# Turning every probability tile by DMA in an attention and MLP block on one Trainium2 core

## The chip, the core and the metric

The kernel runs on one NeuronCore of a Trainium2 chip. Its metric is the device time of one execution in microseconds (us). Three executions of the kernel before took 2775.61, 2779.23 and 2780.73 us, median 2779.23. Comparisons with a changed kernel tell about 0.2% from nothing.

A core has five engines that run their own instruction queues in order: TensorE (PE; its weight loads are listed as PEld), VectorE (DVE), ScalarE (ACT), GpSimd (POOL) and SyncE (SP, which here only issues DMAs). They wait for one another by semaphores. SBUF is the on-chip memory; PSUM holds what TensorE writes.

## The reference

A transformer block over 2048 rows of 576 numbers, modulated by a condition vector `c`:

```python
mod = (silu(c) @ w_mod).reshape(1, 6, 1, 576)
sa, ca, ga, sb, cb, gb = (mod[:, k] for k in range(6))
h = layernorm(x) * (1 + ca) + sa
q = (h @ wq).reshape(1, 2048, 32, 128)         # 32 heads, 16 key/value heads, two heads share one
s = einsum("bhqd,bhkd->bhqk", q, k_last_512) * 128 ** -0.5
o = einsum("bhqk,bhkd->bhqd", softmax(s), v_last_512)
x = x + ga * (o @ wo)
h = layernorm(x) * (1 + cb) + sb
x = x + gb * ((silu(h @ w1) * (h @ w3)) @ w2)  # 4608 hidden columns
```

Everything is fp32 in memory.

## The kernel before

**Precision.** A matrix product is made of fp16 halves: a scaled fp32 value is split into a high half (its fp16 rounding) and a low half (what is left), and a product is high x high + high x low + low x high, three matmuls. Every split costs a copy to fp16 (on ScalarE) and a subtraction (on POOL or VectorE).

**Attention, in slots.** A slot is one head on one block of 512 rows: 32 x 4 = 128 slots, in an order in which most key/value groups do all four blocks at once and some do two and come back later (`uses`, `slots`). Slots come in pairs (`j` = 0 and 1): the two heads of a key/value group on the same block. A slot `i` has four quarters `t`, one for each tile of 128 rows. The loop that starts with `for i in range(n + 2)` writes the work of several slots out in one fixed order, and every engine keeps that order. In slot `i`, quarter `t`, it issues among others:

- `scores(i, t)`: three matmuls (128 x 512) into a PSUM bank of tag "S" (two banks), then VectorE's maximum over each row and the bias for the exponential;
- `weights(i, t)`: ScalarE's exponential `p` of tile `t`, with the row sums into `l`;
- for tiles 0 to 2, `half_high` (ScalarE copies `p` to fp16) and `half_low` (POOL subtracts), both into the tile `hp`, and two quarters later `turn_away`: one DMA transpose on SP's queue writes both halves, turned, into a quarter of `ptw`;
- for tile 3, in quarter 1 of the next slot, `turn`: four 128 x 128 transposes on TensorE into a bank of tag "T", then `turn_high` (ScalarE) and `turn_low` (VectorE) write the halves into `ptw`;
- a third of the next slot's query product (`query`), two groups of the output product of a pair two slots back (`attend_out`, into the bank `E`), and prepared tasks.

At the end of slot `i` `values(i - 1)` makes the value product of the slot before: twelve matmuls, each over all four turned tiles, into a bank of tag "A". So a tile of slot `i - 1` has to be turned by the end of slot `i`.

**The softmax denominator.** `sums` takes the reciprocals of the row sums (VectorE), stores them to DRAM (`row`) and loads them back spread over all partitions (`r`), since the value product comes out with rows along the free axis. `normalize` multiplies, `split_on` makes the halves of the result (copy on ScalarE, subtraction on POOL). `attend_out` sums both heads of the pair in `E` and adds them to `acc` with a scale per key/value group.

**Other work in the slots.** From slot 13 to 123 the MLP's weights are combined, split and stored, mostly on ScalarE and POOL, spread over the quarters (`step_of`); so are the attention's own weights, keys and values (`step_at`). These tasks run in `run(i, t)`, after the quarter's own work. The blocks' normalized rows are turned and modulated (`make_h`) in slots 0 to 1, 8 to 9 and 11 to 12. The MLP (`mlp`) begins in the last slots and fills the rest of the time.

**The opening.** Before slot 0 stand: the loads of the first block, two tables of `w_mod`, two heads of `wq` and one of the keys; the norm; `weigh_mod` and `mod_cols`, which multiply the tables with silu(c) in rows and sum them over partitions by matmuls with ones; peaks and scales (`scale_first`, `scales`); `modulate` for the five chunks of the first block; the first query.

**Buffers.** Every tag has a fixed number of buffers, and a writer waits until the reader of the tile that held its buffer is done: `p` 4, `hf` (with `hp`) 4, `ptw` 2, `raw` 3.

## Time and profile before

| | |
|---|---|
| median of three runs | 2779.23 us |
| profiled execution | 2777.58 us, span 2775.8 us |
| granted TensorE clock | 0.993 |
| busy | PE 2688.3, DVE 1998.5, POOL 1864.7, ACT 1622.7 us |
| bytes moved by DMA | 463 MB |
| first scores / last value product | 38.8 / about 1618 us |

The span is the time from the first to the last instruction of the program; the execution's own time is 1.8 us longer. In the views a row of the timeline is: start and length in us, engine, line, operation, tile written <- tiles read, shapes. A row of groups is: line, engine, operation, tiles, shapes, count | busy us, mean ns of one | idle time of the engine just before them and what ended most of it. A row of waits is: who waited <- for whom: us in total, times, longest. Matmul rows that overlap are merged; their length holds the drain of the pipeline.

### The profile page before, as it was taken

What the parts mean: (1) busy time and instruction counts of PE and PEld (TensorE: products, weight loads), DVE (VectorE), ACT (ScalarE), POOL (GpSimd) and SP (SyncE); (2) the same over time, 40 slices, a digit from 0 to 9 for tenths busy, and PEclk for the clock granted to TensorE, in tenths of its full rate; (3) what the DMA queues carried; (4) which work ended last, traced back from release to release, by engine and by line L of the source; (5) the groups of instructions that cost most, each with busy time, mean ns of one, the idle gap of its engine ahead of it and who ended that gap; (6) DMA issues with size and microseconds to landing.
All of it is one profiled execution on the core that took longest, in us unless ns stands there. A gap on an engine that the chain in (4) does not pass through costs nothing.

```text
span 2775.8 us, 44765 instructions
## 1 busy us (share of the span) xinstructions
PE 2688.3 (97%) x15412; PEld 1513.3 (55%) x15412; DVE 1998.5 (72%) x3556; ACT 1622.7 (58%) x3022; POOL 1864.7 (67%) x1731
## 2 busy tenths in 40 slices
PE   5899999999999999999999999999999999999998
PEld 3455555555555555555555555555555555555555
DVE  7777788877787787887876667777776666566666
ACT  4687777777777878777677635544443333333332
POOL 3567788888788877777669637688873465333435
PEclk8999999999999999999999999999999999999999
DMA  5878778778786888879878935656643434333332
GB/s 164 176 170 190 189 185 188 179 179 189 169 186 165 188 197 189 215 179 208 190 190 223 238 115 170 196 168 201 210 145 108 160 121 128 105 102 110 104 110 78
DMA packets 594420, 463.25 MB, mean 167 GB/s; under 512 B 443152, under 2 KB 472976, under 8 KB 593424
## 3 DMA queue, kind: packets, MB, share of 16 engines
q1 hardware_dynamic: 593584, 460.39, 65.0%
q8 instruction: 121, 1.98, 0.3%
q14 instruction: 107, 0.88, 0.1%
q10 hardware_dynamic: 608, 0.00, 0.0%
HBM read 263.60 MB, written 95.99 MB: 130 GB/s over the span
## 4 chain that ended last, share of the span: by engine, by line
PE 52%; DVE 2%; issue 1%; ACT 1%; POOL 0%; DMA 0%; DVEq 0%; ACTq 0%; POOLq 0%; SPq 0%
PE py L770 15%; PE px L770 11%; PE pe L855 7%; PE pf L855 7%; PE pe L359 3%; PE po L485 3%; PE pss L406 3%; PE pq L348 2%; PE pt L446 0%; PE pq L352 0%; DVE table L410 0%; DVE acc L513 0%; DVE u L955 0%; DVE acc L866 0%; DMA row<-l 0%
## 5 line engine op out<-in xcount | busy, mean ns | idle before, releaser
L460 POOL TENSOR_TENSOR hp<-p,hp 128x512 f16<-128x512 f32 x384 | 448.0, 1169 | 281.0 <-ACT hp L455 156.8
L423 ACT ACTIVATE p<-pss,table,factors 128x512 f32<-128x512 f32 x512 | 396.7, 775 | 357.9 <-DVE table L411 178.2
L770 PEld LDWEIGHTS <-wset 128*128 128x128 f16 x3528 | 344.3, 98 | 336.8 <-issue 3.4
L410 DVE TENSOR_REDUCE table<-pss 128x1 f32<-128x512 f32 x512 | 350.3, 684 | 211.2 <-PE pss L406 207.0
L770 PE MATMUL py<-hset,wset 128*128 128x512 f16 x2016 | 482.4, 379 | 0.0
L359 PE MATMUL pe<-o 128*128 128x288 f16 x3072 | 458.8, 286 | 16.4 <-DVE acc L513 13.9
L406 PE MATMUL pss<-k,qT 128*128 128x512 f16 x1536 | 418.3, 380 | 12.3 <-ACT p L423 9.9
L359 PEld LDWEIGHTS <-o 128*128 128x128 f16 x3072 | 300.3, 98 | 190.1 <-issue 23.4
L485 PE MATMUL po<-ptw,v 128*128 128x512 f16 x1536 | 358.7, 381 | 11.7 <-DVE ptw L475 7.1
L770 PE MATMUL px<-hset,wset 128*128 128x512 f16 x1512 | 361.5, 379 | 1.6 <-ACT p L423 1.6
L348 PE MATMUL pq<-hT,wq 128*128 128x512 f16 x1092 | 281.4, 380 | 1.1 <-DVE hT L216 1.1
L92 POOL TENSOR_TENSOR akv<-u,akv 128x512 f16<-128x512 f32 x141 | 164.8, 1178 | 173.9 <-ACT akv L91 166.0
L455 ACT CAST hp<-p 128x512 f16<-128x512 f32 x384 | 237.4, 618 | 13.1 <-POOL hT L218 0.6
L485 PEld LDWEIGHTS <-v 128*128 128x128 f16 x1536 | 147.6, 98 | 176.5 <-issue 21.0
L855 PEld LDWEIGHTS <-akv 128*128 128x128 f16 x1728 | 169.6, 98 | 93.8 <-issue 4.7
L406 PEld LDWEIGHTS <-qT 128*128 128x128 f16 x1536 | 147.7, 98 | 126.7 <-issue 15.4
L513 DVE SCALAR_TENSOR_TENSOR acc<-pe,factors,acc 128x576 f32<-128x576 f32 x256 | 207.8, 812 | 10.4 <-PE pe L359 10.4
L505 POOL TENSOR_TENSOR o<-on,o 128x512 f16<-128x512 f32 x128 | 150.1, 1173 | 55.8 <-ACT o L504 53.4
L348 PEld LDWEIGHTS <-wq 128*128 128x128 f16 x1104 | 108.6, 98 | 138.5 <-issue 9.0
L849 DVE SCALAR_TENSOR_TENSOR acc<-pf,table,acc 128x576 f32<-128x576 f32 x140 | 113.5, 811 | 80.3 <-PE pf L855 80.3
L950 ACT COPY u<-py 128x512 f32<-128x512 f32 x72 | 42.1, 585 | 202.2 <-PE py L770 200.3
L943 ACT ACTIVATE s<-s,table 128x512 f32<-128x512 f32 x72 | 52.0, 722 | 174.2 <-DVE s L942 174.2
(230 smaller groups left out, 4780.3 us busy)
## 6 DMA issues: line engine op xcount, KB each, us to landing
wset<-wd SPq DMA_DIRECT2D x213, 320.0 KB, 3.2
r<-row SPq DMA_DIRECT2D x128, 256.0 KB, 4.1
oset<-od SPq DMA_DIRECT2D x106, 288.0 KB, 3.2
wraw<-in_w SPq DMA_DIRECT2D x36, 768.0 KB, 5.6
wd<-wmade SPq DMA_DIRECT2D x75, 320.0 KB, 3.3
wset<-wd SPq DMA_DIRECT2D x71, 160.0 KB, 2.3
w2raw<-in_w SPq DMA_DIRECT2D x19, 576.0 KB, 5.1
wd<-ring SPq DMA_DIRECT2D x33, 320.0 KB, 2.9
```

The lines of the kernel that those rows point to most:

```text
L92: eng.tensor_sub(halves[:, 1], src, halves[:, 0])
L348: nc.tensor.matmul(ps, w[:, k // 2, m, :], hT[:, DC + m if k == 1 else m, :], start=s == 0, stop=False)
L359: nc.tensor.matmul(E[:, h, :HALF], o[:, x, rows], w[:, y, h * HALF : (h + 1) * HALF], start=first and n == 0, stop=last and n == 2,)
L406: nc.tensor.matmul(pss, q[:, x, rows], k[:, y, :], start=n == 0, stop=n == 2)
L410: nc.vector.tensor_reduce(nm[:, 0:1], pss, axis=AX.X, op=ALU.max, negate=True)
L423: nc.scalar.activation(p, pss, AF.Exp, bias=nm[:, 1:2], scale=factor, accum_out=st["l"][:, t : t + 1])
L455: nc.scalar.copy(hp[:, 0, :], state[i]["p", t])
L460: nc.gpsimd.tensor_sub(hp[:, 1, :], state[i].pop(("p", t)), hp[:, 0, :])
L485: nc.tensor.matmul(po, v[:, x, c, :], pt[:, y, c, :], start=c == 0 and n == 0, stop=c == KC - 1 and n == 2)
L513: nc.vector.scalar_tensor_tensor(a, E[:, :, :HALF], factors[:, uses[u][0], 2:3], a, op0=ALU.mult, op1=ALU.add)
L770: nc.tensor.matmul(ps, w[:, a, :], h[:, b, :], start=start and n == 0, stop=stop and n == 6, skip_group_check=True)
L855: nc.tensor.matmul(ps[:, h, :HALF], a[:, rows], w[:, b, :], start=m == 0, stop=m == 2)
```

## The change

It has five parts.

1. **Tile 3 is turned by DMA too.** `turn`, `turn_high` and `turn_low` are gone. `half_high` runs for all four tiles, and `turn_away` has four transposes a slot, those of tiles 2 and 3 in quarters 0 and 1 of the next slot.
2. **The low half is a quarter later.** `half_low(i, t - 1)` stands at the start of quarter `t`, behind the tasks of quarter `t - 1`; that of tile 3 at the start of the next slot.
3. **Scores in four banks.** The two "T" banks are free of `turn`; even tiles' scores go there, odd tiles' to "S".
4. **A ratio of sums for a pair.** Head 0 of a pair is no longer divided by its row sum: `take_first` (ScalarE) and one VectorE instruction split its value product straight from PSUM. Head 1 is multiplied with the ratio of the two sums; the store and the spread by DMA happen for this head alone. The division by head 0's sum moves into the factor of `attend_out`, a column per tile.
5. **The opening.** The two tables come in turned by the host (`w_cols`) with `c` repeated in all partitions, so that the modulation vectors are sums along the free axis (`weigh_col`); two heads of `wq` and the keys load ahead of the second table. The peaks of the weights are found before it, TensorE runs matmuls on unused data (`warm`), half of the normalized rows are made on ScalarE. `modulate_first` makes all high halves first, and `project_first` multiplies with them first. For the other blocks `modulate` makes one fp32 result and lets POOL make both halves.

On TensorE, in quarter 1 of the slot whose first scores start at 809.58 us of the profile: before (`pt` is the turned tile's bank, `pe` the bank E, `o` and `qT` halves of the output and the query),

```order
L359 LDWEIGHTS o
L359 MATMUL pe<-o 128x288
L446 MATMUL pt<-ident,p 128x128 x4
L406 LDWEIGHTS qT
L406 MATMUL pss<-k,qT 128x512
```

and now

```order
L434 LDWEIGHTS o
L434 MATMUL pe<-o 128x288
L484 LDWEIGHTS qT
L484 MATMUL pss<-k,qT 128x512
L484 LDWEIGHTS qT
```

The four transposes are gone and the scores follow the output product at once.

On POOL, around the last quarter of the slot whose fourth scores start at 984.89 us: before (`hp` are low halves, of tile 2 first and of the next slot's tile 0 last; `wraw` and `wmade` are MLP weights, `o` the split of an attention output),

```order
L460 TENSOR_TENSOR hp<-p,hp 128x512
L685 TENSOR_TENSOR wraw<-wraw 128x384
L686 TENSOR_TENSOR wraw<-wraw 128x384
L687 TENSOR_TENSOR wraw<-wraw 128x384
L505 TENSOR_TENSOR o<-on,o 128x512
L692 TENSOR_TENSOR wmade<-wraw,wmade 128x2x256
L693 TENSOR_TENSOR wmade<-wraw,wmade 64x2x128
L695 TENSOR_TENSOR wraw<-wraw 128x384
L460 TENSOR_TENSOR hp<-p,hp 128x512
```

and now, from the low half of tile 1 on,

```order
L531 TENSOR_TENSOR hp<-p,hp 128x512
L769 TENSOR_TENSOR wraw<-wraw 128x384
L770 TENSOR_TENSOR wraw<-wraw 128x384
L771 TENSOR_TENSOR wraw<-wraw 128x384
L531 TENSOR_TENSOR hp<-p,hp 128x512
L589 TENSOR_TENSOR o<-on,o 128x512
L776 TENSOR_TENSOR wmade<-wraw,wmade 128x2x256
L777 TENSOR_TENSOR wmade<-wraw,wmade 64x2x128
L779 TENSOR_TENSOR wraw<-wraw 128x384
L531 TENSOR_TENSOR hp<-p,hp 128x512
```

The low half of tile 2 has moved behind three weight instructions, and that of tile 3, which is new, stands behind the output's split and three more.

On SP's queue, from the same slot as the first place on: before (`ptw` a turned tile, `row` and `r` the reciprocals out and back, `od` MLP weights, `oraw` and `wraw` loads),

```order
L467 DMA_TRANSPOSE ptw<-hp 128x8x128
L642 DMA od_172<-omade 128x1152
L436 DMA r<-row_9460 128x512
L467 DMA_TRANSPOSE ptw<-hp 128x8x128
L287 DMA oraw<-in_wo 128x1152
L467 DMA_TRANSPOSE ptw<-hp 128x8x128
```

and now

```order
L538 DMA_TRANSPOSE ptw<-hp 128x8x128
L350 DMA oraw<-in_wo 128x1152
L538 DMA_TRANSPOSE ptw<-hp 128x8x128
L726 DMA od_175<-omade 128x576
L538 DMA_TRANSPOSE ptw<-hp 128x8x128
L516 DMA row_9204<-l 128x4
```

Four transposes a slot stand there, and a `row` with its `r` in every second slot.

The core of the diff:

```diff
-        pss = bank("S", "pss")
+        pss = bank("S", "pss") if t % 2 else t_bank()
...
     def sums(i, step):
 
+        u, j, b = slots[i]
         st = state[i]
+        if j == 0:
+            return
+        first, both, up, ratio = (st["l"][:, lo * ST : hi * ST] for lo, hi in ((0, 1), (0, 2), (2, 4), (4, 5)))
         if step == 0:
-            nc.vector.reciprocal(st["l"][:, ST:], st["l"][:, :ST])
+            nc.vector.reciprocal(up, both)
+            nc.vector.scalar_tensor_tensor(ratio, first, O_DOWN, up[:, ST:], op0=ALU.mult, op1=ALU.mult)
         elif step == 1:
             st["row"] = dram.tile([P, ST], F32, name=f"row{i}")
-            nc.sync.dma_start(st["row"], st["l"][:, ST:])
+            nc.sync.dma_start(st["row"], ratio)
...
+    def take_first(i):
+        st = state[i]
+        o = st["o"] = new_o(i)
+        nc.scalar.activation(o[:, 0, :], st["po"], AF.Copy, scale=O_DOWN)
+
     def normalize(i):
         st = state[i]
         po = st.pop("po")
+        if slots[i][1] == 0:
+            o = st["o"]
+            nc.vector.scalar_tensor_tensor(o[:, 1, :], po, O_DOWN, o[:, 0, :], op0=ALU.mult, op1=ALU.subtract)
+            return
...
-        for h in (high, hf):
-            if on_vector:
-                nc.vector.tensor_scalar(h, ps, g, s, op0=ALU.mult, op1=ALU.add)
-            else:
-                nc.scalar.activation(h, ps, AF.Identity, bias=s, scale=g)
-        eng = nc.vector if on_vector else nc.gpsimd
+        if on_vector:
+            nc.vector.tensor_scalar(hf, ps, g, s, op0=ALU.mult, op1=ALU.add)
+        else:
+            nc.scalar.activation(hf, ps, AF.Identity, bias=s, scale=g)
+        nc.gpsimd.tensor_copy(high, hf)
...
+    def weigh_col(wm, k, m, on_vector):
+        w, to = wm[m], mod_a[:, k, m : m + 1]
+        if on_vector:
+            nc.vector.scalar_tensor_tensor(w, w, 1.0, c_row, op0=ALU.mult, op1=ALU.mult, accum_out=to)
+        else:
+            nc.gpsimd.tensor_mul(w, w, c_row)
+            nc.scalar.activation(w, w, AF.Copy, accum_out=to)
...
     load_x(0)
-    load(wms, 0, load_mod, 0, wrest[:, 0])
-    load(wms, 1, load_mod, 1, wrest[:, 1])
+    load(wms, 0, load_cols, 0, wrest[:, 0])
     load(wqs, (0, 0), load_in, wq, 0)
     load(keys, 0, load_kv, k_cache, 0)
     load(wqs, (0, 1), load_in, wq, 1)
+    load(wms, 1, load_cols, 1, wrest[:, 1])
...
         for t in range(ST):
+            if t and i < n:
+                half_low(i, t - 1)
+            if t == 0 and 1 <= i <= n:
+                half_low(i - 1, ST - 1)
             if t > 1 and i < n:
                 turn_away(i, t - 2)
-            if t == 0 and 1 <= i <= n:
-                turn_away(i - 1, 2)
-            slot, tile = (i - 1 if t == 1 else n, ST - 1)
-            if 0 <= slot < n:
-                turn(slot, tile)
+            if t < 2 and 1 <= i <= n:
+                turn_away(i - 1, t + 2)
             if i < n:
                 scores(i, t)
             if 2 <= i <= n and t == 1:
                 normalize(i - 2)
-            if 1 <= i <= n and t == 2:
-                turn_low(i - 1, ST - 1)
...
-            if t < 3 and i < n:
+            if i < n:
                 half_high(i, t)
-                half_low(i, t)
-            if t == 1 and 1 <= i <= n:
-                turn_high(i - 1, ST - 1)
+            if 2 <= i <= n + 1 and t == 0 and slots[i - 2][1] == 0:
+                take_first(i - 2)
```

214 lines of the change are left out of this document (144 added, 70 removed).

## The prediction, made before the changed kernel was run

> **What bounds the kernel now.** I read the page first, then the busy times in stretches of eight slots (start and end, length, then each engine's busy time in the order PE, PEld, DVE, ACT, POOL, and clock, DMA share, GB/s), then what TensorE waits for.
>
> ```profile
> PE 2688.3 (97%) x15412; PEld 1513.3 (55%) x15412; DVE 1998.5 (72%) x3556; ACT 1622.7 (58%) x3022; POOL 1864.7 (67%) x1731
> PE   5899999999999999999999999999999999999998
> POOL 3567788888788877777669637688873465333435
> PEclk8999999999999999999999999999999999999999
> ...
> 554.80:650.20 95.40, 93.28 (x538) 52.23 (x536) 73.73 (x150) 76.30 (x147) 85.52 (x82) 1.00 0.74 174
> 1225.40:1318.10 92.70, 92.70 (x535) 52.23 (x534) 69.86 (x143) 70.24 (x137) 66.96 (x61) 1.00 0.90 195
> 811.99:823.57 11.58, 11.58 (x68) 6.52 (x67) 10.04 (x19) 9.52 (x20) 11.50 (x11) 1.00 0.95 162
> ```
>
> TensorE is busy for 97% of the span at full clock. The last row is one slot: 11.58 us, all of them busy. The row above it is eight slots in 92.70 us, again 11.59 each and no idle time. So a slot costs what TensorE has to do in it, unless something is late. But POOL is close behind: 85.52 of 95.40 us in the first of these stretches.
>
> ```profile
> PE pe L359 <- DVE acc L513: 13.9, 15, 2.0
> PE pss L406 <- ACT p L423: 9.9, 16, 1.7
> PE po L485 <- DVE ptw L475: 7.1, 12, 2.9
> PE po L485 <- DMA ptw<-hp: 3.4, 4, 1.8
> ```
>
> These are TensorE's waits that belong to the attention slots (total, times, longest). They are small: the tiles turned by DMA are late four times in 384. This is the row to keep in mind, since the change takes away the reserve behind it.
>
> **The gain: the fourth tile's transposes.**
>
> ```profile
> 811.68 0.53 PE L359 MATMUL pe<-o 128*128 128x288 f16 x3
> 812.04 0.60 PE L446 MATMUL pt<-ident,p 128*128 128x128 f32 x4
> 812.48 0.81 PE L406 MATMUL pss<-k,qT 128*128 128x512 f16 x3
> ```
>
> The next work starts 812.48 - 812.04 = 0.44 us after the four transposes start (the 0.60 holds the drain, which overlaps). 128 slots x 0.44 = **56.3 us** of TensorE, and since TensorE sets the slot this is on the path. A slot becomes 11.58 - 0.44 = 11.14 us if nothing is late. With the transposes go ScalarE's copy and VectorE's subtraction of that tile; ScalarE gets a half-precision copy instead, as for the other tiles:
>
> ```profile
> L450 ACT CAST ptw<-pt 128x512 f16<-128x512 f32 x128 | 74.0, 578 | 0.6 <-PE pt L446 0.6
> L475 DVE TENSOR_TENSOR ptw<-pt,ptw 128x512 f16<-128x512 f32 x128 | 87.6, 684 | 26.4 <-ACT ptw L450 25.6 <-issue 0.2
> L455 ACT CAST hp<-p 128x512 f16<-128x512 f32 x384 | 237.4, 618 | 13.1 <-POOL hT L218 0.6
> ```
>
> VectorE gets 0.68 us a slot freer and ScalarE 0.04 fuller; neither holds the slot (10.04 and 9.52 of 11.58 us in the row of one slot), so I price this at 0. Should either hold it after all, see the last rival.
>
> **Old waits.** VectorE's late subtraction (7.1 us) is gone with its instruction. Four score banks instead of two take most of the 9.9 us in which scores waited for an exponential. The two waits add up to 17.0; I take **15 us**, and between 8 and 20. The 13.9 us behind the accumulation stay: its bank is the same.
>
> **The opening.**
>
> ```profile
> 11.02 0.78 ACT L136 ACTIVATE wm<-wm,sc 128x576 f32<-128x576 f32 x1 [2.08 <-DMA wm<-in_w_mod]
> 15.15 0.78 ACT L136 ACTIVATE wm<-wm,sc 128x576 f32<-128x576 f32 x1 [2.69 <-DMA wm<-in_w_mod]
> 15.71 1.67 DVE L134 SCALAR_TENSOR_TENSOR wm<-wm,sc 128x576 f32<-128x576 f32 x2
> 22.50 0.15 DVE L992 TENSOR_REDUCE us<-shift_a 128x1 f32<-128x5 f32 x1
> 25.36 0.22 DVE L1004 TENSOR_SCALAR gain_a<-gain_a,us 128x5 f32<-128x5 f32 x1
> 28.48 0.76 ACT L213 ACTIVATE hT<-pt,shift_a,gain_a 128x512 f16<-128x512 f32 x1
> 29.14 0.77 ACT L213 ACTIVATE hf<-pt,shift_a,gain_a 128x512 f32<-128x512 f32 x1
> 37.52 0.59 PE L352 MATMUL pe<-hT,wq 128*128 128x512 f16 x2
> 38.80 1.46 PE L406 MATMUL pss<-k,qT 128*128 128x512 f16 x3 [0.69 <-ACT qT L390]
> ```
>
> The first scores start at 38.80. The two tables of modulation weights land 4.13 us apart (11.02 and 15.15; by their tiles' shapes 1152 + 144 KB, so 314 KB per us). The change puts 896 KB (two heads of wq, one of keys) ahead of the second, and some 440 KB more of c and tail rows: it lands (896 + 440) / 314 = 4.3 us later, near 19.4. Five weighted sums on VectorE at 0.83 (half of 1.67) end at 23.6, the scaling chain (22.50 to 25.58) at 26.7, so h starts 1.8 us earlier than 28.48. From there high halves come first, and the last low half waits for four passes on ScalarE (29.14 - 28.48 = 0.66 apart) and three subtractions on POOL (about 1.2 each, as the low halves quoted below): 26.7 + 2.6 + 3.6 = 32.9, and 38.80 - 37.52 = 1.3 for the last matmuls and the copy of q make 34.2. That is 4.6 us earlier; I take **5**, between 0 and 8. A loss is possible too: for blocks 1 to 3 the change makes the high half on POOL, an instruction that the trace doesn't have; nearest is the subtraction of the same shape, 1.2, so at most 6 us of POOL a block. POOL's slices there are 3 to 7 tenths full and hide it, unless block 1 comes late by as much (+6).
>
> **What the change makes late: the fourth tile.** The value product of a slot reads all four turned tiles. It runs at the end of the next slot.
>
> ```profile
> 817.19 0.81 PE L406 MATMUL pss<-k,qT 128*128 128x512 f16 x3
> 818.57 2.75 PE L485 MATMUL po<-ptw,v 128*128 128x512 f16 x12
> 830.20 1.03 PE L485 MATMUL po<-ptw,v 128*128 128x512 f16 x4
> ```
>
> The scores of tile 3 start at 817.19, its value product at 830.20: 13.0 us, in the changed slot 12.5. Before, that tile needed no DMA. Now in these 12.5 us stand the exponential, the high half on ScalarE, the low half on POOL behind all POOL work of that quarter (this is the quarter slot later), and the transfer:
>
> ```profile
> 821.15 1.60 POOL L505 TENSOR_TENSOR o<-on,o 128x512 f16<-128x512 f32 x1
> 822.71 1.28 POOL L724 TENSOR_TENSOR omade<-w2raw,omade 128x576 f16<-128x576 f32 x1
> ...
> L460 POOL TENSOR_TENSOR hp<-p,hp 128x512 f16<-128x512 f32 x384 | 448.0, 1169 | 281.0 <-ACT hp L455 156.8 <-issue 85.5 <-DVE table L411 14.0
> ...
> DMA to landing us min/median/max: 3.0/3.9/9.5
> ```
>
> In this slot the quarter's POOL work ends at 823.99, 6.8 us after the scores. The low half (1.17, the group's row) and the landing of such a transfer (median 3.9, the last line of the view of the turned tile) make 11.9, and about 0.5 more since ScalarE now has one copy more ahead of that work: 12.4. It just fits. In a slot with more to do in that quarter it doesn't:
>
> ```profile
> 984.89 0.81 PE L406 MATMUL pss<-k,qT 128*128 128x512 f16 x3
> ...
> 992.40 1.16 POOL L692 TENSOR_TENSOR wmade<-wraw,wmade 128x512 f16<-128x512 f32 x1
> 993.63 0.67 POOL L693 TENSOR_TENSOR wmade<-wraw,wmade 64x256 f16<-64x256 f32 x1
> 994.38 1.00 POOL L695 TENSOR_TENSOR wraw<-wraw 128x384 f32<-128x384 f32 x1
> ```
>
> POOL is free at 995.38, 10.5 us after the scores; with 1.17 and 3.9 that is 15.6, 3.1 too late, and TensorE stands.
>
> How often? I counted, in the changed order of POOL, the work between the third and the fourth low half of each slot, with the durations of these rows and their like. 89 of 127 slots have at most 2.1 us there (the slot of 821.15 has 2.4): they fit, price 0. 23 have 2.3 to 3.0, so up to half a microsecond too much: 23 x 0.5 = 11.5. 15 have 3.6 us or more (the slot of 984.89 has 3.8): between 1.2 (its least excess over 2.4) and 3.1 late; I take 2.0, since the 3.1 holds work of the quarter before: 15 x 2.0 = 30. Together **+41.5 us**. A stall gives the next chain just as much time, so neighbours don't add; and if ScalarE lags less than here, the 23 cost nothing: between 15 and 75.
>
> **POOL's total.** A slot gets one low half more (1.17) and half an output split less (0.59): +0.58. In the stretch of 554.80 that is 85.5 + 4.7 = 90.2 us, while TensorE, without its 2.1 us of idle time (95.40 - 93.28) and the transposes (3.5), needs 89.8. Only this stretch is over-full, by 0.4. But the waits of low halves for ScalarE's copy (156.8 us in the POOL row) go away where the copy is a quarter old. I take **+5**, between 0 and 15.
>
> **DMA and SyncE.** Each slot has four transfers of 256 KB now (three turned tiles, one row of reciprocals spread over partitions) and gets 4.5, since the ratio needs the spread for one head of two. At 174 to 195 GB/s and 11.6 to 11.9 us a slot moves some 2.2 MB; 128 KB more is 6%, in a slot 4% shorter: the share goes from 0.74 to 0.90 of the stretches to 0.82 to 1.0. The stretch at 0.90 ran without idle time, so I price it at 0; were the landing 1 us later, the 38 slots over the edge would slip by 1 us, +38.
>
> [...]
>
> **The sum**, against the profiled execution's 2777.6 (span 2775.8; the median of the three runs is 2779.2, 0.06% above): 2777.6 - 56.3 - 15 - 5 + 41.5 + 5 = **2748**, 1.1% faster.
>
> **The rivals.** *TensorE stays full* (25%). Lateness shrinks as TensorE stands still, and POOL no longer waits for ScalarE; then 2777.6 - 76.3 + 5 = 2706. For it: the 156.8 us, and the slots at exactly 11.58. Against it: 3.1 us too late in the slot of 984.89. *Every fourth tile is late* (17%). Then TensorE waits at each value product. The mean of the two slots shown is (12.4 + 15.6) / 2 = 14.0, 1.5 over; a slower landing under the fuller queue adds 0.4. Two slots share a chain, so half of 1.9 is lost per slot, 0.95: 128 x 0.95 = 122 us against the 76 won, 2823. It turns to slower from 0.6 us a slot on. For it: POOL at 11.50 of 11.58 in the slot above; against it: the count, 89 slots with little work there. [...] *The transposes weren't on the path* (8%): VectorE or ScalarE hold the slot at 11.58 anyway and only the opening gains, 2772. Against it: 92.70 of 92.70.
>
> **How the numbers follow.** The forecast has 50%, with a range of its own of 2722 to 2770 (the 41.5 between 15 and 65). The range reaches to the first rival's 2706 and, upwards, to half of the second: 2706 to 2796. What a measurement here can tell from no change is about 0.2%, 5.6 us. Faster: nearly all of the forecast (0.48), the first rival (0.25), a small part of the last: 0.74. Same: most of the last and the forecast's edge, 0.09. Slower: the second rival, 0.17.
>
> **What would show it.** The L446 group is gone and the slots without extra POOL work take 11.14 us. TensorE's waits list po on the transfers of ptw at 30 to 60 us instead of 3.4, longest about 3, in the slots with weight splits in the last quarter. Scores waiting for exponentials fall under 3 us. The first scores start near 34. Wrong it would be if po hardly waits (first rival), or if it waits in nearly every slot, or if the landing of the transfers goes from 3.9 to 5 or more.

## The result: 4.9% slower, and the profile after

Four executions of the changed kernel took 2909.4 to 2915.1 us, median 2912.5; the kernel before took 2777.4 beside them. The ratio is 1.0485 (interval 1.0473 to 1.0497). The forecast was 2748, its range 2706 to 2796: the sign is wrong, and the time lies outside the range. The profiled execution has a span of 2913.3 us against 2775.8, so 137.5 us have to be found.

The page of the changed kernel, engines and slices:

```profile
PE 2685.4 (92%) x14894; PEld 1465.8 (50%) x14894; DVE 1970.2 (68%) x3491; ACT 1631.9 (56%) x3013; POOL 1947.5 (67%) x1812
...
PE   6799989989889988998999889999999999999998
...
POOL 5578778888888787676676844678875455443345
PEclk8999999999999999999999999999999999999999
```

TensorE's share went from 97 to 92%, and the gaps are in the slices of the attention, not in the MLP. Two stretches of it, before (start and end, length, then busy times of PE, PEld, DVE, ACT and POOL, clock, DMA share, GB/s):

```profile
554.78:747.36 192.58, 187.04 (x1075) 104.35 (x1073) 148.07 (x298) 149.13 (x289) 166.84 (x161) 1.00 0.77 176
1177.36:1318.13 140.77, 139.88 (x803) 78.22 (x801) 109.22 (x221) 107.47 (x211) 105.48 (x96) 1.00 0.88 195
```

and the same slots (16 with the densest weight work, then 12 with half of it) after, with a slot that waits for nothing:

```profile
586.09:800.26 214.17, 186.84 (x1011) 98.41 (x1009) 145.54 (x292) 150.48 (x289) 176.35 (x169) 0.97 0.73 169
1276.70:1434.01 157.31, 141.05 (x756) 73.94 (x753) 106.26 (x216) 109.34 (x211) 110.26 (x101) 0.96 0.84 181
```

```profile
301.88:313.02 11.14, 11.14 (x64) 6.07 (x62) 9.36 (x19) 10.31 (x20) 8.34 (x8) 1.00 0.94 239
```

The slot of 11.14 us that the prediction worked out exists, but only about one slot in five is like it (25 of 127 take under 11.3 us). The mean is 214.17 / 16 = 13.4 us where POOL is fullest and 157.31 / 12 = 13.1 where it has least to do (before 12.0 and 11.7). POOL's load hardly matters for the loss: the light slots lose as much as the full ones. The granted clock fell to 0.96 too.

TensorE's groups before, those of output product, scores and value product:

```profile
L359 PE MATMUL pe<-o 128*128 128x288 f16 x3072 | 458.8, 286 | 16.4 <-DVE acc L513 13.9 <-DVE us L257 2.3
L406 PE MATMUL pss<-k,qT 128*128 128x512 f16 x1536 | 418.3, 380 | 12.3 <-ACT p L423 9.9 <-ACT qT L390 1.1 <-DVE qT L396 0.7
L485 PE MATMUL po<-ptw,v 128*128 128x512 f16 x1536 | 358.7, 381 | 11.7 <-DVE ptw L475 7.1 <-DMA ptw<-hp 3.4 <-ACT hp L455 0.5
```

and after:

```profile
L434 PE MATMUL pe<-o 128*128 128x288 f16 x3072 | 460.6, 287 | 33.9 <-DVE acc L597 26.1 <-DVE table L1177 5.0 <-DVE table L1148 2.0
L551 PE MATMUL po<-ptw,v 128*128 128x512 f16 x1536 | 395.4, 412 | 143.2 <-DMA ptw<-hp 96.8 <-issue 27.1 <-DMA row<-l 16.0
...
L484 PE MATMUL pt<-k,qT 128*128 128x512 f16 x768 | 212.6, 384 | 8.7 <-ACT qT L468 4.0 <-DVE hf L250 1.7 <-DVE qT L474 1.5
```

The value product waits 143.2 us instead of 11.7. It also takes longer once it runs: 412 ns against 381 for the same matmul. One such place, TensorE after:

```profile
364.09 0.90 PE L434 MATMUL pe<-o 128*128 128x288 f16 x6
369.78 4.86 PE L551 MATMUL po<-ptw,v 128*128 128x512 f16 x12 [4.79 <-DMA ptw<-hp]
374.48 0.81 PE L484 MATMUL pt<-k,qT 128*128 128x512 f16 x3
```

The granted clock in those microseconds (length, PE busy, clock, DMA share, GB/s):

```profile
368.00:370.00 2.00, 0.22 (x1) 0.50 1.17 250
370.00:372.00 2.00, 2.00 (x6) 0.50 0.58 103
372.00:374.00 2.00, 2.00 (x6) 0.50 1.22 139
374.00:376.00 2.00, 2.00 (x11) 0.98 1.10 277
```

After a wait of 4.79 us the twelve matmuls run at half the clock and take 4.86 us instead of 2.75. The tile they waited for, tile 3 of its slot, had its scores on TensorE and its high half on ScalarE at

```profile
350.89 0.81 PE L484 MATMUL pss<-k,qT 128*128 128x512 f16 x3
```

```profile
354.54 0.62 ACT L526 CAST hp<-p 128x512 f16<-128x512 f32 x1
```

This is what POOL did meanwhile (a part of it, in order of time):

```profile
356.47 1.41 POOL L820 TENSOR_TENSOR w2raw<-w2raw,gate_b 128x576 f32<-128x576 f32 x1
357.83 1.16 POOL L531 TENSOR_TENSOR hp<-p,hp 128x512 f16<-128x512 f32 x1
358.95 0.80 POOL L822 TENSOR_TENSOR w2raw<-w2raw 128x288 f32<-128x288 f32 x1
359.82 0.80 POOL L823 TENSOR_TENSOR w2raw<-w2raw 128x288 f32<-128x288 f32 x1
360.57 1.16 POOL L531 TENSOR_TENSOR hp<-p,hp 128x512 f16<-128x512 f32 x1
361.69 1.17 POOL L589 TENSOR_TENSOR o<-on,o 128x512 f16<-128x512 f32 x1
362.81 0.81 POOL L825 TENSOR_TENSOR w2raw<-w2raw 128x288 f32<-128x288 f32 x1
363.56 0.81 POOL L828 TENSOR_TENSOR w2raw<-w2raw 128x288 f32<-128x288 f32 x1
364.31 1.16 POOL L531 TENSOR_TENSOR hp<-p,hp 128x512 f16<-128x512 f32 x1
```

The three L531 rows are the low halves of tiles 1, 2 and 3. Tile 3's is the last, 9.15 us after its high half was done (354.54 + 0.62 = 355.16). POOL is never idle, but it does other things first: the quarters' tasks, and two low halves that are themselves late for the same reason. From the single instructions of the trace: a low half that could start waits 3.3 us on average for POOL (before 1.3). Tile 3's starts 8.8 us after its scores in the median, and the tile lands at 14.85 us (quartiles 13.1 and 16.2), where 12.5 were allowed. The transfers are not slower (3.9 us in the median before; the view of the turned tile, after):

```profile
DMA to landing us min/median/max: 3.0/3.6/8.2
```

**Where 137.5 us went**, by these rows and by the starts of TensorE's instructions. "Half speed" is what matmuls lose that start over 1.4 times their line's usual distance after the one before, with no gap between: 289 of them, mostly 427 ns apart instead of 216, against 50 before. "Drains": 50 more stalls, each with the end of a pipelined matmul bared, an estimated 0.17 us (381 ns that a matmul of the value product takes in the rows before, less the 215 between two starts in the trace).

| | us |
|---|---|
| opening (first scores at 33.49 instead of 38.80) | -5.3 |
| transposes on TensorE | -56.3 |
| value product's waits, 143.2 - 11.7 | +131.5 |
| output bank's waits, 33.9 - 16.4 | +17.5 |
| scores' waits, 8.7 - 12.3 | -3.6 |
| half speed, 53.8 - 7.8 | +46.0 |
| drains | +8.5 |
| sum (137.5 measured) | +138.3 |

The granted clock confirms the half-speed row: in the attention 107.6 us of TensorE's work (12.5 before) fell into stretches at half clock, and half of that, 53.8 us (6.3 before), is lost.

**Who is late.** In the changed kernel the value product stalls in 62 of the 128 slots, 2.3 us in the mean, and at every one of these stalls tile 3 lands last. Where it stalls, tile 3's low half had waited 4.8 us for POOL in the mean, counted from the end of its high half, in the other slots 2.7. The time from the scores to the end of the high half (5.3 and 5.1 us), the time from the low half's end to the transfer's issue (0.8 and 0.8) and the transfer itself (4.0 and 3.7) hardly differ. So what is late is the low half.

### The profile page after: what moved, and what is told of

The parts are those of the page before. It is cut to its first block, busy times and chain, and to the rows that moved or that the text cites. A ratio compares the mean times of both kernels' runs of the same rounds, so it can differ in the third digit from the quotient of the medians.

```text
span 2913.3 us, 43728 instructions
## 1 busy us (share of the span) xinstructions
PE 2685.4 (92%) x14894; PEld 1465.8 (50%) x14894; DVE 1970.2 (68%) x3491; ACT 1631.9 (56%) x3013; POOL 1947.5 (67%) x1812
## 5 line engine op out<-in xcount | busy, mean ns | idle before, releaser
L531 POOL TENSOR_TENSOR hp<-p,hp 128x512 f16<-128x512 f32 x512 | 594.2, 1169 | 89.6 <-ACT hp L526 57.3
L551 PE MATMUL po<-ptw,v 128*128 128x512 f16 x1536 | 395.4, 412 | 143.2 <-DMA ptw<-hp 96.8
L434 PE MATMUL pe<-o 128*128 128x288 f16 x3072 | 460.6, 287 | 33.9 <-DVE acc L597 26.1
L501 ACT ACTIVATE p<-pt,table,factors 128x512 f32<-128x512 f32 x256 | 198.5, 776 | 380.1 <-DVE table L489 357.3
L526 ACT CAST hp<-p 128x512 f16<-128x512 f32 x512 | 316.4, 618 | 88.5 <-DMA ptw<-hp 72.1
L551 PEld LDWEIGHTS <-v 128*128 128x128 f16 x1536 | 154.2, 104 | 343.8 <-issue 151.1
L488 DVE TENSOR_REDUCE table<-pss 128x1 f32<-128x512 f32 x256 | 175.9, 687 | 157.9 <-PE pss L484 156.4
L488 DVE TENSOR_REDUCE table<-pt 128x1 f32<-128x512 f32 x256 | 174.4, 681 | 152.6 <-PE pt L484 152.3
L484 PE MATMUL pt<-k,qT 128*128 128x512 f16 x768 | 212.6, 384 | 8.7 <-ACT qT L468 4.0
L501 ACT ACTIVATE p<-pss,table,factors 128x512 f32<-128x512 f32 x256 | 198.1, 774 | 37.9 <-DVE table L489 31.8
L597 DVE SCALAR_TENSOR_TENSOR acc<-pe,l,acc 128x576 f32<-128x576 f32 x256 | 207.5, 810 | 16.0 <-PE pe L434 15.4
L484 PE MATMUL pss<-k,qT 128*128 128x512 f16 x768 | 210.0, 383 | 0.0
L474 DVE SCALAR_TENSOR_TENSOR qT<-pq,qT 128x512 f16<-128x512 f32 x127 | 87.6, 690 | 127.7 <-ACT qT L468 127.6
```

Source lines behind the costliest of these rows:

```text
L434: nc.tensor.matmul(E[:, h, :HALF], o[:, x, rows], w[:, y, h * HALF : (h + 1) * HALF], start=first and n == 0, stop=last and n == 2,)
L484: nc.tensor.matmul(pss, q[:, x, rows], k[:, y, :], start=n == 0, stop=n == 2)
L488: nc.vector.tensor_reduce(nm[:, 0:1], pss, axis=AX.X, op=ALU.max, negate=True)
L501: nc.scalar.activation(p, pss, AF.Exp, bias=nm[:, 1:2], scale=factor, accum_out=st["l"][:, j * ST + t : j * ST + t + 1])
L526: nc.scalar.copy(hp[:, 0, :], state[i]["p", t])
L531: nc.gpsimd.tensor_sub(hp[:, 1, :], state[i].pop(("p", t)), hp[:, 0, :])
```

## The experiments

The theories, as the expectations call them: **A**, the later place of the low halves is the main cause; **B**, the ring of four `hp` buffers; **C**, turning tile 3 by DMA takes too long wherever its low half stands; **D**, the engines and queues are too full in total, or other parts of the change cost time. Later, for what low_own left: **E**, tile 3's low half waits for POOL; **F**, transfers and SyncE's queue are too slow; **G**, a slot loses half of what tile 3 is over its deadline; **H**, the engines keep their order and the delays add up; **I**, **J**, **K**, the room on POOL, ScalarE or VectorE holds the slot.

All runs in one table; each is described below. Median and ratio to the kernel before (with interval), then TensorE's waits in the attention by what waited (value product, output product, scores), and its loss at half speed, in us.

| run | median | ratio | product | output | scores | half speed |
|---|---|---|---|---|---|---|
| before | 2778 | | 11.7 | 14.0 | 11.6 | 7.8 |
| the change | 2912.5 | 1.0485 (1.0473-1.0497) | 143.2 | 31.4 | 8.0 | 53.8 |
| low_own | 2802.6 | 1.0086 (1.0071-1.0101) | 53.2 | 36.7 | 8.7 | 27.2 |
| ring5 | 2914.3 | 1.0484 (1.0463-1.0504) | 141.5 | 31.1 | 5.6 | 57.6 |
| values_later | 2929.8 | 1.0547 (1.0532-1.0563) | 2.8 | 2.1 | 181.8 | 43.9 |
| before_late | 2845.2 | 1.0240 (1.0224-1.0255) | 37.3 | 37.1 | 9.4 | 21.8 |
| own_tensor | 2769.2 | 0.9963 (0.9950-0.9976) | 8.4 | 13.6 | 10.7 | 10.2 |
| own_dve3 | 2959.7 | 1.0654 (1.0636-1.0672) | 14.1 | 198.3 | 18.3 | 36.3 |
| own_early | 2854.5 | 1.0271 (1.0255-1.0286) | 48.0 | 75.6 | 8.9 | 37.2 |
| own_later | 2828.8 | 1.0179 (1.0163-1.0194) | 6.2 | 34.4 | 71.7 | 19.8 |
| late3 | 2842.5 | 1.0232 (1.0215-1.0250) | 100.3 | 25.6 | 6.9 | 36.7 |
| own_split | 2803.1 | 1.0076 (1.0059-1.0093) | 34.0 | 54.3 | 9.5 | 26.8 |
| after_split | 2888.9 | 1.0387 (1.0372-1.0403) | 88.0 | 63.6 | 11.0 | 33.2 |
| own_banks2 | 2800.1 | 1.0069 (1.0054-1.0084) | 55.3 | 22.4 | 27.2 | 20.2 |
| own_no_low3 | 2760.1 | 0.9931 (0.9916-0.9946) | 32.1 | 38.6 | 14.7 | 23.6 |
| own_few10 | 2805.2 | 1.0103 (1.0085-1.0120) | 57.5 | 31.9 | 7.9 | 28.4 |
| tensor_few10 | 2767.3 | 0.9959 (0.9944-0.9974) | 9.1 | 18.8 | 12.0 | 11.3 |
| after_fill | 2933.2 | 1.0555 (1.0539-1.0571) | 78.1 | 14.1 | 5.3 | 25.6 |
| own_less_act | 2798.3 | 1.0066 (1.0050-1.0083) | 54.9 | 35.4 | 6.6 | 28.6 |
| own_less_dve | 2785.2 | 1.0020 (1.0009-1.0032) | 52.2 | 28.2 | 7.7 | 21.9 |

### Which part costs: the later low halves, or tile 3 by DMA

**low_own**: the low halves back in their own quarter, nothing else.

```diff
-            if t and i < n:
-                half_low(i, t - 1)
-            if t == 0 and 1 <= i <= n:
-                half_low(i - 1, ST - 1)
...
                 half_high(i, t)
+                half_low(i, t)
```

> The changed kernel with one part undone: each low half stands again in its own quarter, right behind the high half, ahead of the quarter's tasks; tile 3's too. Four tiles by DMA, four banks, ratio and opening stay. Theory A (the later place of the low halves is the main cause: their start after the scores went from 5.2-5.5 us to 7.8-8.8 in the median): most of the loss comes back, 2720 to 2790 us, TensorE's waits for the turned tiles fall from 139.9 us (transfers 96.8, issue 27.1, row 16.0) to under 60. Theory B (the ring of four hp buffers, now used by four tiles a slot, couples ScalarE to the transfers): part of it, 2830 to 2880, since the transfers still hold the ring. Theory C (a tile 3 that goes by DMA is too late wherever its low half stands): above 2850. Theory D (POOL and the queues are too full in total): above 2850.

2802.6 us: 110 of the 134 us that the change cost came back, a little less than theory A said, and far from the numbers of the others. Tile 3 now lands 12.7 us after its scores in the median (14.85 in the change), and TensorE's waits for it are

```profile
PE po L551 <- DMA ptw<-hp: 36.5, 25, 4.8
PE pe L434 <- DVE acc L597: 26.5, 25, 2.7
...
PE po L551 <- issue: 6.8, 4, 2.7
PE po L551 <- DMA row<-l: 6.1, 1, 6.1
```

**before_late**: the kernel before with this part alone, three tiles by DMA.

```diff
+            if t and i < n:
+                half_low(i, t - 1)
             if t > 1 and i < n:
                 turn_away(i, t - 2)
...
                 half_high(i, t)
-                half_low(i, t)
```

> The kernel before with the second part of the change alone: the low halves of tiles 0 to 2 a quarter later, behind the quarter's tasks; tile 3 is turned by TensorE as before. Theory A: tile 2 lands near 14.7 us after its scores instead of 11.8, against 15.2 allowed, so that a third of the slots waits for it by 1 to 3 us: 2800 to 2850 us, TensorE's wait for the transfers 20 to 60 us instead of 3.4. Theory C: within 0.4% of before (2766 to 2788), since tile 2 has a quarter more time than tile 3. Theory B: up to 10 us slower. D: unchanged, the work is the same.

67 us slower, with no tile 3 in it. Tile 2 lands at 14.35 us (before 11.80), nearly as expected, though its product wait grew by only 26 us; the output product's wait, which no theory named, grew nearly as much, by 23:

```profile
PE pe L359 <- DVE acc L513: 38.5, 33, 3.2
PE po L485 <- DMA ptw<-hp: 26.7, 13, 4.7
```

So the later place costs in both kernels. **late3**: low_own, with tile 3's low half alone a quarter later.

```diff
-                half_low(i, t)
+            if i < n and t < ST - 1:
+                half_low(i, t)
...
+            if t == 0 and 1 <= i <= n:
+                half_low(i - 1, ST - 1)
```

> Four tiles by DMA, low halves of tiles 0 to 2 in their own quarter, only tile 3's low half a quarter later as in the changed kernel. Theory G (a slot loses half of what tile 3's way from scores to landing is over 12.5 us, as two slots share a chain; the change's 14.85 us cost (14.85 - 12.5) / 2 = 1.2 us a slot): tile 3's own lateness does most of it, 2850 to 2900. Theory H (all four late low halves count alike, since POOL and ScalarE keep their order and the delay adds up): about a quarter of the 110 us between the two runs, 2815 to 2845.

40 of the 110 us. Tile 3 alone costs more than the quarter that theory H gave it, but most of the loss comes only with the other three, as theory H has it. They act through tile 3: it lands last at every stall of the product in both kernels, and its low half starts 6.3 us after its scores in low_own, 8.2 in late3 and 8.7 in the change (medians). The last 0.5 us a slot fit the other 70 us (0.55 us a slot): POOL keeps its order, so a late half makes the next one later.

**own_tensor**: parts 1 to 3 of the change undone; ratio and opening stay.

```diff
-        pss = bank("S", "pss") if t % 2 else t_bank()
+        pss = bank("S", "pss")
...
-            if t < 2 and 1 <= i <= n:
-                turn_away(i - 1, t + 2)
+            if t == 0 and 1 <= i <= n:
+                turn_away(i - 1, 2)
+            slot, tile = (i - 1 if t == 1 else n, ST - 1)
+            if 0 <= slot < n:
+                turn(slot, tile)
```

> The changed kernel with its first three parts undone: tile 3 is turned by TensorE, low halves stand in their own quarter, scores use two banks. What is left of the change is the ratio of sums for a pair and the new opening. Theory A with C (late low halves cost most, the turn of tile 3 by DMA the rest): the opening's 5.7 us are all that moves, 2766 to 2776. Theory D (the other parts of the change cost time too, by SyncE, VectorE or the new high half on POOL): 2783 or more.

2769.2 us, 0.4% faster than before and in the range of A and C. Ratio and opening are worth 9.5 us; the first scores start 6.1 us earlier, so the opening is most of it. This version beats both kernels. Against it low_own is 33 us slower, although TensorE has 56 us less to do: that is the price of tile 3 by DMA. **own_banks2** shows that the four banks aren't it: low_own with two.

```diff
-        pss = bank("S", "pss") if t % 2 else t_bank()
+        pss = bank("S", "pss")
```

> Low halves in their own quarter, four tiles by DMA, and the scores in two banks as before the change (the other two lie idle). If the four banks are harmless or help: 2803 to 2830, with scores waiting for exponentials again (before: 9.9 us). If they cost time, because VectorE's maxima and ScalarE's exponentials may now fall further behind TensorE: 2770 to 2795.

2800.1 against 2802.6, intervals overlapping; the time lies between the two ranges that were expected. Scores wait 18 us more and the output product 14 us less.

### The rival: a ring of four buffers

In the changed kernel ScalarE waits for a landing before it may write the next high half (the ring has four buffers and a slot now uses four):

```profile
ACT hp L526 <- DMA ptw<-hp: 72.1, 56, 4.1
```

**ring5** gives it a fifth:

```diff
-HF, STORE = 4, 3
+HF, STORE = 5, 3
...
-            st["r"] = pool.tile([P, P, ST], F32, tag="kv", name="r", bufs=8)
+            st["r"] = pool.tile([P, P, ST], F32, tag="kv", name="r", bufs=7)
...
```

> The changed kernel with five hp buffers instead of four; one of the eight buffers of the tag kv is given up for the space. Nothing else. Theory A: within 15 us of the changed kernel (2912), since the high halves that wait for a transfer (72.1 us in 56 waits) are a consequence of late transfers. Theory B: those waits are what feeds the lateness; without them at least a third of the loss comes back, below 2865, and ScalarE's wait for ptw<-hp falls under 10 us. C and D: no change.

The wait is gone and the time is the same: theory B falls.

```profile
ACT hp L526 <- DMA ptw<-hp: 5.6, 5, 1.9
```

### More time for the tile

**values_later**: the change with the value product behind the query product of the next slot's first quarter.

```diff
...
+            if 2 <= i <= n and t == 0:
+                values(i - 2)
...
-        if 1 <= i <= n:
-            values(i - 1)
...
```

> The changed kernel with the value product a quarter of a slot later (in quarter 0 of the slot after next, behind the query product; the split of the result moves by a quarter with it), so that every turned tile has about 2.9 us more. All work is the same. Theories A, B and C (the tiles are late, the engines not too full): tile 3 landed at 14.85 us after its scores in the median against 12.5 allowed; with 15.4 allowed a stall is left in a third of the slots or fewer, 2700 to 2780 us. Theory D (POOL, ScalarE or the queues can't do the work in 11.14 us a slot): the lateness grows by as much as it is given, above 2850.

Slower, 2929.8, and yet the value product waits no longer (2.8 us). TensorE now waits for the copy of the next query, which the value product had covered at the end of each slot:

```profile
PE pt L484 <- ACT qT L468: 151.1, 119, 4.7
```

The run doesn't tell C from D, since it bares something else. **own_later** tries to avoid that: low_own, the product as late, and the query product finished a quarter earlier.

```diff
-                query(i + 1, t)
+                for part in (((0,), (1, 2), ()) if i > 12 else ((0,), (1,), (2,)))[t]:
+                    query(i + 1, part)
+            if 2 <= i <= n and t == 0:
+                values(i - 2)
...
```

> Low halves in their own quarter, four tiles by DMA, and the value product a quarter later (2.9 us more for every tile); so that the copy of the next query isn't bared, as it was in the run with the later product, the query product of slots 13 and on is done by the end of quarter 1. All theories of lateness (A, C, E, F): tile 3 landed at 12.7 us in the median and 16.1 in the worst twentieth, against 15.4 allowed: product waits under 10 us, 2710 to 2750. Theory D (an engine or queue can't do 11.14 us a slot): above 2790.

2828.8: product waits fell to 6.2 as expected, but scores wait 71.7 us for the query's halves. The work now lies in quarters 0 and 1 of the slot, so this too compares two orders, not only two deadlines. By its number the run lies where the expectation put theory D (above 2790), which it therefore doesn't exclude for what low_own left. **own_split** gives the low half 1.7 us more and moves no other engine's work: tile 3 goes in two transfers, and the product takes its high halves first.

```diff
-        for c in range(KC):
-            for n, (x, y) in enumerate(((0, 0), (1, 0), (0, 1))):
+        for n, (x, y) in enumerate(((0, 0), (1, 0), (0, 1))):
+            for c in range(KC):
...
+                turn_part(i - 1, 3, 0)
+            if t == 1 and 1 <= i <= n:
+                turn_part(i - 1, 3, 1)
...
```

> Low halves in their own quarter, and tile 3 turned in two transfers: its high half as soon as ScalarE has made it, its low half as before; the value product multiplies with the high halves first, so that the low half is wanted 8 matmuls (8 x 0.216 = 1.7 us) later. One more transfer of half the size in each slot. Theory G: the product's waits fall from 53.2 us to under 20, and half the half-speed matmuls go, 2745 to 2780 us. Theory F (the queue and the transfers are the limit): one more transfer makes it worse, above 2803. Theory H: 2790 to 2803, as the engines' order holds the slot.

2803.1, nothing gained: product waits fell by 19 us, and the output product's grew by 18. The same in the changed kernel, **after_split**:

> The changed kernel, low halves late, with tile 3 in two transfers and the high halves first in the value product, as in the run before. Theory G: tile 3's low half is wanted 1.7 us later, a slot loses (14.85 - 12.5 - 1.7) / 2 = 0.3 us instead of 1.2, less than that for the other tiles, and fewer matmuls run at half speed: 2790 to 2850 us. Theory F or H: 2890 to 2930.

2888.9: 24 us gained, with 55 us less at the product and 32 more at the output. More than half of what the product no longer loses (32 of 55 us here, 18 of 19 in own_split) is lost a few matmuls on, where TensorE waits for the output bank, mostly for VectorE to empty it. Theory G, in which the product's deadline is all, falls: own_split lies at the upper end of H's range, after_split just under it.

### What else holds tile 3

**own_dve3**: low_own with tile 3's low half on VectorE; **own_early**: low_own with every transfer a quarter earlier in SyncE's queue.

```diff
-        nc.gpsimd.tensor_sub(hp[:, 1, :], state[i].pop(("p", t)), hp[:, 0, :])
+        eng = nc.vector if t == ST - 1 else nc.gpsimd
+        eng.tensor_sub(hp[:, 1, :], state[i].pop(("p", t)), hp[:, 0, :])
```

```diff
-            if t > 1 and i < n:
-                turn_away(i, t - 2)
-            if t < 2 and 1 <= i <= n:
-                turn_away(i - 1, t + 2)
+            if t > 0 and i < n:
+                turn_away(i, t - 1)
+            if t < 1 and 1 <= i <= n:
+                turn_away(i - 1, ST - 1)
```

> Low halves in their own quarter, four tiles by DMA, and tile 3's low half on VectorE (which the change freed of a subtraction of the same size) instead of POOL. Theory E (what is left of the loss is tile 3's low half waiting for POOL: in the run with low halves in their own quarter it starts 6.3 us after its scores in the median, 1.35 after the high half, and 11.2 in the worst twentieth): tile 3 lands 1 to 3 us earlier and POOL has 1.2 us a slot less; 2735 to 2775 us. Theory F (the transfers themselves and SP's queue are too slow for 12.5 us): 2790 to 2805. If VectorE is now the one that is late: above 2805.

> Low halves in their own quarter, four tiles by DMA, and each transfer a quarter earlier in SyncE's queue (one quarter after its tile's scores instead of two). Theory F (the queue's order holds the transfers: they start 0.6 to 1.0 us after the low half is done): up to 1 us a slot earlier, 2765 to 2790. Theory E: the start is bound by the low half, 2790 to 2805. If the transfers, waiting for POOL, hold up the loads behind them: above 2810.

Both are much slower, 2959.7 and 2854.5, for reasons of order, so neither decides between E and F. In own_dve3 VectorE stands in each of the 128 slots until ScalarE's copy is there, and the output bank behind it isn't emptied:

```profile
DVE hp L532 <- ACT hp L526: 169.1, 128, 8.9
```

In own_early the transfers wait at the head of SyncE's queue for POOL (566.3 us in the three largest of these waits, 502.0 in low_own), and behind them stands the spread of the ratio, for which VectorE then waits (4.9 us in low_own):

```profile
DVE on L572 <- DMA r<-row: 45.9, 23, 5.1
```

Whether any one engine has too little room in a slot was asked by taking work away from low_own. **own_no_low3** leaves tile 3's low half out of everything; **own_few10** moves 12 items of weight work into the MLP's time (and **tensor_few10** the same from own_tensor); **own_less_act** leaves out the scaling of the MLP's weights on ScalarE, **own_less_dve** the maxima over them on VectorE.

```diff
...
+                w = SB if y == 0 else SB - P
                 nc.tensor.matmul(
-                    po, v[:, x, c, :], pt[:, y, c, :], ...
+                    po[:, :w], v[:, x, c, :], pt[:, y, c, :w], ...
...
```

```diff
-    FEW = 8
+    FEW = 10
...
```

```diff
-                for part in range(2):
-                    step_at(step - 2 + part, in_put, w, part)
...
-                step_at(step - 8, out_put, w, 0)
-                step_at(step - 7, out_put, w, 1)
```

```diff
+        if f >= NF - FEW:
             nc.vector.tensor_reduce(
...
```

> Low halves in their own quarter, four tiles by DMA; tile 3's low half is left out altogether: no subtraction on POOL (1.17 us a slot), a transfer of the high half alone, and the value product leaves out tile 3's quarter in its four low matmuls (4 x 0.054 = 0.2 us a slot of TensorE). Theory I (POOL has too little room: 10.8 to 11.25 us of work in slots that should take 11.14): the loss goes and most of the 56 us appear, 2700 to 2750. Theory H (the order of ScalarE and VectorE, which keep all their work, holds the slot): 2765 to 2790 with output-bank waits as they are (36.7 us).

> Low halves in their own quarter, four tiles by DMA, and 12 of the 168 items of MLP weight work moved out of the slots into the MLP's time, where ScalarE and POOL are half idle (7% of some 5 us a slot of POOL and ScalarE work, 0.3 us). Theory I: 0.2 to 0.3 us a slot over some 108 slots, 2770 to 2785, if the MLP takes no longer. If room isn't the limit: 2797 to 2808.

> Ratio and opening alone (three tiles by DMA, tile 3 by TensorE, low halves in their own quarter), and the same 12 items moved into the MLP's time. TensorE sets the slot there (43.5 us idle in 1574), so 0 to 15 us: 2755 to 2770. Above 2775 if the MLP pays for it.

> Low halves in their own quarter, four tiles by DMA; left out is the scaling of the MLP's weights on ScalarE that stands in the slots (56 instructions of 0.931 us and 28 of 0.773, 73.8 us in all; the output is no longer the reference's). Theory J (ScalarE's room holds the slot): 40 to 75 us come back, 2730 to 2765. Theory K (VectorE's does: exponentials wait 324.0 us for its maxima): under 20 us, 2785 to 2803. Theory I (POOL's room): under 20 us.

> Low halves in their own quarter, four tiles by DMA; left out are the maxima over the MLP's weights on VectorE that stand in the slots (56 instructions of 0.944 us and 14 of 1.344, 71.7 us in all; the weights' scale is then a constant). Theory K: 35 to 70 us come back, 2735 to 2770, and the output bank's waits fall from 36.7 us to under 15. Theories J and I: under 20 us, 2785 to 2803.

Against low_own: POOL's 1.17 us a slot gave 42 us, between the ranges of I and H; of it an estimated 28 are TensorE's own shorter product (128 x 4 x 0.054, a quarter of the 0.216 us between two matmuls of 512 columns). ScalarE's 73.8 us gave 4; VectorE's 71.7 gave 17; 12 items of all of them gave nothing. own_tensor gains nothing from them either (2767.3 against 2769.2, intervals overlapping). Theories I and J fall, and K too: 17 us where at least 35 were expected, with the output product still waiting 28.2. No single engine's amount of work, taken away alone, gives back the 33 us.

### Half speed and idle time

**after_fill**: the change with five useless matmuls ahead of each value product.

```diff
         po = bank("A", "po")
+        for _ in range(5):
+            nc.tensor.matmul(po, v[:, 0, 0, :], v[:, 0].rearrange("p c d -> p (c d)"), start=True, stop=True)
```

> The changed kernel with five useless matmuls (5 x 0.216 = 1.1 us, 138 us in all) ahead of each value product, overwritten by it; they wait for nothing of the tiles. If half speed follows from TensorE's own idle time: idle stretches get 1.1 us shorter, those over 2 us fall from 40 to under 20 and the loss at half speed from 53.8 us to under 30, so that 138 us of added work cost less than 60: 2900 to 2970. If half speed has another cause (power, the transfers): it stays near 50 us, 2970 or more.

138 us of added work cost 21. Stalls over 2 us fell from 40 to 17, idle time in the attention from 194.8 to 111.7 us, and the loss at half speed from 53.8 to 25.6. So most of the added work filled time in which TensorE stood anyway (83 us), and 28 us came back from the clock. Tile 3 lands as late as in the change (14.7 us in the median against 14.85), so it isn't the transfers: half speed follows from TensorE's own idle time.

## Why the prediction was wrong

**The gain** was right: a slot without waits takes 11.14 us. **The opening** was right: 33.49 us for the first scores (34.2 worked out), 5.3 us against 5. **The transfers** were right to be priced at 0: 3.6 us to land, not 5. **Old waits**: scores no longer wait for exponentials, though some now wait for the query's copy (3.6 us gained) and VectorE's 7.1 are gone with the instruction; 10.7 against 15, within its bounds. **POOL's total** is 1947.5 - 1864.7 = 82.8 us more, 0.65 a slot (0.58 worked out), and no run shows it to be the limit.

**The step that failed is the count of late slots**, +41.5 us with 15 to 75, where the product's waits grew by 131.5. It priced a slot by POOL's work between the third and the fourth low half alone, and took the time at which POOL gets there from one slot (free 6.8 us after tile 3's scores, 12.4 of 12.5 used). The counting itself came true: in the changed kernel 89 slots have under 2 us of work in that gap, 24 have 2.3 to 3.1 and 15 have 3.8 or more. But the 89 that were priced at 0 hold 38 of the 62 stalls and 85 of the 143 us; the 24 lose 33 us (11.5 worked out) and the 15 lose 24 (30 worked out). In the 89, too, POOL is free for tile 3's low half only 7.7 us after its scores in the median. What the count left out is the work that POOL is still behind with when it comes to the gap.

The profile before had this already: over 127 slots POOL reaches the place of the new low half 7.95 us after the fourth scores in the median (quartiles 6.6 and 10.2), and only 38 slots are as early as the one that served as the measure. With the prediction's own 1.17 and 3.9 the median makes 13.0, over the 12.5 allowed. The change adds to it, since the work ahead of tile 3's low half now includes the late halves of tiles 1 and 2 and the tasks ahead of those, as the rows from 356.47 on show. low_own shows the size, 110 us, and late3 that 70 of them come only with the other three tiles; on the kernel before, those three alone cost 67.

A small term was missing besides: from the end of tile 3's low half to the issue of its transfer on SyncE's queue pass 0.8 us in the mean (0.03 in the median), where the sum had nothing.

**VectorE and ScalarE at 0** failed too: the output product waits 17.5 us longer. In own_split it grows by what the product's shrinks. When TensorE stands, VectorE's and ScalarE's work bunches behind the stall; that is how I read it, but no run isolates it, so it is not shown.

**What was not in the sum at all** is the half-speed clock, +46.0 us, a third of the loss. Every term priced a stall by its length.

**The rival that came nearest** is "every fourth tile is late", given 17%. It had a chain 1.9 us late in every second slot, 0.95 us a slot; measured are 62 stalls in 128 slots, 2.3 us each, and (143.2 - 11.7) / 128 = 1.03 us a slot. That it fits so well is in part luck, since 0.4 of its 1.9 us was a slower landing that didn't come (3.6 us against 3.9). Its time, 2823, is 92 us short of the profiled 2915.1: half speed 46.0, the output bank 17.5, drains 8.5, 9.5 more in the product's waits, and gains of 65.2 us (transposes 56.3, opening 5.3, scores 3.6) where it had 76.3. What the prediction had against it, the count of light slots, is the step that failed.

**Open** is what holds the slot in low_own, where tile 3 goes by DMA with its low half in time. Its loss to own_tensor is found in the value product (+45 us), the output product (+23) and half speed (+17), against 56 won. The banks, the product's deadline and the work of any one engine are each excluded as its sole cause. The ring was tested only in the changed kernel, and the place of the transfers only in own_early, which bared another wait; both stay open here. Two stretches of low_own, 16 of the densest slots and the 12 light ones:

```profile
560.82:756.63 195.81, 182.91 (x1010) 97.47 (x1008) 145.55 (x289) 150.72 (x289) 175.62 (x169) 0.99 0.80 185
1194.90:1335.90 141.00, 135.22 (x756) 72.68 (x753) 106.32 (x216) 108.76 (x210) 110.97 (x101) 1.00 0.91 205
```

In the first a slot takes 12.2 us, with 11.0 of POOL, 9.4 of ScalarE and 9.1 of VectorE, where 11.14 were hoped for. That the three are nearly full at once and hold one another up in their fixed orders is one reading. It can't be all: in the light slots POOL has 9.2 us, and a slot still takes 11.75, no less than before the change (11.73), though TensorE has less to do. In the 36 slots of low_own in which the product stalls, tile 3's low half had waited 3.2 us for POOL in the mean, in the other 92 slots 1.2; so theory E stands for the product's part. What holds the rest is not shown.

## What to carry to other kernels

An instruction that is moved behind other work on its engine is late by everything that engine is still behind with, and where several of its kind move, each is late by the others too (here tile 3's alone cost 40 us, all four 110): measure when the engine gets there over all slots, not at the one slot in which it fits and not by the work in one gap. Price a stall of the bounding engine at more than its length (here 46.0 us at half speed came on top of 131.5 us of the product's waits), and ask what it covers: the value product's place at the slot's end hid the query's copy, for which TensorE waited 151.1 us once it was bared. Work taken from the bounding engine is won only as far as the others have their results ready earlier: low_own took 56 us from TensorE and lost 33 against own_tensor.

## What the hardware showed that was not expected

TensorE's stalls have a second price. In the changed kernel, none of the 27 stalls of the value product of 0.3 to 2 us is followed by matmuls at half speed, 7 of 16 from 2 to 3 us are, and 16 of 17 above that; these then run some 9 matmuls at 427 ns instead of 216 before full speed returns, a little under 2 us lost. The granted clock in such a place is 0.50 (from 368 us on in the rows above). Length alone does not divide the stalls: seven of 2.0 to 2.8 us are caught, and one of 3.65 us is not; what else decides is not shown. After a caught stall 7 to 14 matmuls in a row start over 1.4 times the usual distance after the one before, 2.9 to 5.9 us in all. The prediction had stalls of up to 3.1 us in its own working and priced none of this.
